# RWKV-5 recurrence into a SoLU feed-forward block on one core: w loaded from ScalarE's queue, one join behind the states' updates, and another order of the last steps

## The chip, the core and the metric

The kernel runs on one core of one Trainium2 chip. The metric is the device time in microseconds of one execution. The engines are named as the profile names them: PE is TensorE (PEld its weight loads), DVE is VectorE, ACT is ScalarE, POOL is GpSimd, SP is SyncE, which issues nearly all transfers here.

## What is computed

Shapes: batch 4, 8 heads, 768 steps, head width 48; the feed-forward block has 3072 rows of 384 and an inner width of 1024. All is float32, except that the feed-forward weights arrive as 64-bit words and are converted in the kernel.

```python
for t in range(S):                                   # B, H, S, D = 4, 8, 768, 48
    kt, vt, rt = k[:, :, t], v[:, :, t], r[:, :, t]
    cur = einsum('bhd,bhe->bhde', u * kt, vt)
    y[:, :, t] = einsum('bhd,bhde->bhe', rt, state + cur)
    state = w * state + einsum('bhd,bhe->bhde', kt, vt)
x = y.transpose(0, 2, 1, 3).reshape(B * S, H * D)    # 3072 x 384
h = x @ w_in                                         # 3072 x 1024
solu = h * softmax(h)
ln = (solu - mean(solu)) / sqrt(var(solu) + 1e-6) * g_ln
out = ln @ w_out                                     # 3072 x 384
```

## The kernel before

The sequence is cut into 6 chunks of 128 steps; with 4 batches this makes N = 24 units, and unit i carries the state of unit i - 4 on. A unit's 128 rows go through three stages that run at the same time for different units: the recurrence for units i and i + 1, the inner product and softmax for unit j = i - 2, and the output product for unit l = i - 7. The order of every engine is written out by hand (`manual_schedule`): each engine executes its instructions in the order in which the program lists them, and waits on semaphores for those of other engines. Tiles of one pool and tag take turns in a few buffers, and an instruction that writes into a buffer waits until the tile before is done with. The tag "raw" (6 buffers) holds loads of weights at first, later the halves described below.

**Start.** `w` (4 x 2 x 48) is loaded into `wq` by a transfer that POOL issues (L493); `u` into one row of `u_bc` by one that ACT issues (L496). POOL then makes an identity matrix, with which PE does three warming products (`spin`, L619), transposes w (`wd_ps`, L636) and spreads u over all rows by a product with ones (`u_ps`, L638, copied by ACT, L639). From `wd_ps` DVE builds powers `pw` and, by doubling, the table `tab` of decays for 128 steps (L643 to L654). The first products of POOL (`wide` L1313, `weigh` L734 and L735, `decay_k` L721), the scaling of the transposed r and k (L779, L790) and `kdec` come from this table.

**Middle.** From unit 9 on, k and r are turned by a transposing transfer of 16-bit halves: ACT splits the words into halves (L1133, L1139), SP issues the transfer (L1107), and DVE joins the halves again (`join_rk`, L1112, into a tile `big`). The normalised rows go the same way: `halve_ln` (ACT, L1118), L1107, `join_ln` (DVE, L1112). In each turn of the loop (i = 9, 11, 13, 15, 17) `first` is unit i + 2 and `second` unit i + 3. From l = 4 (`SEVEN`) two output blocks are computed together with seven block products instead of eight; this needs sums of rows (`row_sums_12`, DVE, L1192 and L1193; `row_sums_34`, L1197 and L1198) and differences of weights (`weight_sums`, L1182). The third difference overwrites weights in place, in the turn i = 11, on DVE. In such a turn `both_a` to `both_d` issue PE's block products (L1202) and what takes them out of PSUM: copies by ACT (L1219, L1230, L1235, L1278) and additions by DVE (L1228; `both_c`: L1262 and L1267). A block product that writes a bank again waits for the copy or addition that read it. `unit_a` (DVE, L1049 and L1053) multiplies the inner rows by their softmax, after ACT's exponential (L977); `update` (DVE, L949) writes the states.

**End.** After the loops the rest is listed step by step. For the last unit `unit_b` squares on ACT (L1061), `deviation` computes the variance, its power -1/2, and a scale and a shift on POOL:

```python
nc.gpsimd.tensor_scalar(out=var, ...)                # L1073
nc.gpsimd.tensor_tensor(out=rstd, ..., op=ALU.pow)   # L1075
nc.gpsimd.tensor_scalar(out=scale, ...)              # L1079
nc.gpsimd.tensor_tensor(out=shift, ...)              # L1081
```

`normalise` applies them on ACT (L1093), and halving, transposing and joining follow before the output products. Beside this, `check_next` reads the weights once more: it issues one load (SP, L524) and has ACT take the magnitudes of the load before (`mag`, L582); `check_least` takes their minimum on DVE (L590), and `compare_sums` (L691 to L700) and `check_sums` (one product `n_ps`, L706) turn all of it into a flag.

Of the kernel before, what the change touches and what calls it, by code (L numbers as in the profile page):

```python
# [12 lines left out]
ALU = mybir.AluOpType  # L13
# [386 lines left out]
def direct_path(  # L400
# [29 lines left out]
    nc = tc.nc  # L430
    B, H, S, D = r.shape
# [58 lines left out]
    w_out_sb = const.tile([128, KF, dm], F32, name="w_out_sb")  # L490
    decays = const.tile([128, HP], F32, name="decays")

    nc.gpsimd.dma_start(out=wq[:, :, 0:D], in_=w.rearrange("(a q) d -> a q d", q=2))  # L493
    nc.vector.memset(wq[:, :, D:], 1.0)
    u_row = u_bc[0:1].rearrange("p h d -> p (h d)")
    nc.scalar.dma_start(out=u_row, in_=u.rearrange("h d -> (h d)").unsqueeze(0))  # L496
# [571 lines left out]
        unit_a(i)  # L1068
        unit_b(i)

    def deviation(i, j):
        ss, var, rstd = (stats[:, n, i:j] for n in (2, 3, 4))
        nc.gpsimd.tensor_scalar(out=var, in0=ss, scalar1=1.0 / dff, scalar2=1e-6 * dff ** 2,  # L1073
                                op0=ALU.mult, op1=ALU.add)
        nc.gpsimd.tensor_tensor(out=rstd, in0=var, in1=neg_half.to_broadcast([128, j - i]), op=ALU.pow)  # L1075
        i = max(i, SEVEN)
        if i < j:
            tot, shift, scale, rstd = (stats[:, n, i:j] for n in (1, 2, 3, 4))
            nc.gpsimd.tensor_scalar(out=scale, in0=rstd, scalar1=-float(dff), scalar2=1.0,  # L1079
                                    op0=ALU.mult, op1=ALU.mult)  # L1080
            nc.gpsimd.tensor_tensor(out=shift, in0=tot, in1=rstd, op=ALU.mult)  # L1081

    def normalise_late(i):
        if SEVEN <= i < N:
# [4 lines left out]
    def normalise(i):  # L1089

        if SEVEN <= i < N:
            solu = live[i]["solu"]
            nc.scalar.activation(out=solu, in_=solu, func=ACT.Identity,  # L1093
                                 scale=stats[:, 3, i : i + 1], bias=stats[:, 2, i : i + 1])
# [26 lines left out]
    def join_ln(i):  # L1121
        X = live[i]
        if i not in ROOM:
            X["lnT"] = fpool.tile([128, KF, 128], F32, name="lnT")
        else:
            X["lnT"] = bigs[ROOM[i]].rearrange("p (f t) -> p f t", f=KF)
        join(X["lnT"], X["turned"])
# [19 lines left out]
    def join_rk(i):  # L1147
        X = factors(i)
        join(X["rk"].rearrange("p e a t -> p (e a) t"), X["turned"])
# [96 lines left out]
    def both_c_sum(i, also=False):  # L1246
        X = live[i]
        o2 = X["o2"]
        nc.vector.tensor_tensor(out=o2[:, right], in0=X["a"], in1=o2[:, right], op=ALU.add)
        X["summed"] = True  # L1250
        if also:
            o = X["o"]
            nc.vector.tensor_tensor(out=o[:, right], in0=X["e"], in1=o[:, right], op=ALU.add)
            X["summed"] = 2

    def both_c(i):
        X, Y = live.pop(i), live.pop(i + 1)
        ending[i] = X
        o, o2, a, e = (X[n] for n in ("o", "o2", "a", "e"))
        rows, rows2 = (out[ds(b * S + c * T, T)] for b, c in (units[i], units[i + 1]))  # L1260
        if not X.get("summed"):
            nc.vector.tensor_tensor(out=o2[:, right], in0=a, in1=o2[:, right], op=ALU.add)  # L1262
        block(a, Y["lnT"][:, KH:KF], sums_w[4])
        if i + 2 == N:
            nc.sync.dma_start(out=rows2[:, right], in_=o2[:, right])
        if X.get("summed") != 2:
            nc.vector.tensor_tensor(out=o[:, right], in0=e, in1=o[:, right], op=ALU.add)  # L1267
        nc.sync.dma_start(out=rows, in_=o)

    def both_d(i):  # L1270
        X = ending.pop(i)
        (b, c), o2, a = units[i + 1], X["o2"], X["a"]
        rows2 = out[ds(b * S + c * T, T)]
        if i + 2 == N:
            nc.vector.tensor_copy(out=o2[:, left], in_=a)
            nc.sync.dma_start(out=rows2[:, left], in_=o2[:, left])
        else:
            nc.scalar.copy(out=o2[:, left], in_=a)  # L1278
            nc.sync.dma_start(out=rows2, in_=o2)
# [177 lines left out]
    i = LA + LO  # L1457
# [42 lines left out]
    for i in range(LA + LO + 2, ELEVEN, 2):  # L1500
        j, l = i - LA, i - LA - LO
        seven = l >= SEVEN
        for n in (i + 6, i + 7):
            if n < N:
                load(n, "kr")
        for n in (i + 3, i + 4):
            if n < N:
                load(n, "v")
        deviation(j - 2, j)
        first, second = ([n] if n < N else [] for n in (i + 2, i + 3))  # L1510
        for n in first + second:
            diagonal(n)
        if SEVEN <= l <= EARLY:
            row_sums_34(l, nc.gpsimd)
        if l < SEVEN:
            decay(i + 4)
        elif i + 4 < N:
            weigh(i + 4, nc.gpsimd)
        decay(i + 5)
        if SEVEN <= l + 2 and i + 6 < N:  # L1520
            decay_k(i + 6)
            decay_r(i + 6)
        ffn_in(j)
        attend([i, i + 1])
        unit_a(j)
        second_pair = i == LA + LO + 2
        if l == EARLY + 4:
            check_next()
        if l < EARLY + 4:
            halve_ln(l + 2)  # L1530
        else:
            normalise(l + 3)
        if seven:
            both_a(l)
        if l == EARLY + 4:
            halve_ln(l + 3)
        for n in (i, i + 1):
            if n < N:
                place(n)
        if i >= CHECKED and l < EARLY + 4:  # L1540
            check_next()
        unit_b(j)
        if l == EARLY + 4:
            deviation(j, j + 1)
        if l <= EARLY:
            normalise(l + 3)
        take([i, i + 1])
        if second_pair:
            halve_rk(i + 3)
        if seven:  # L1550
            take_a(l, "DVE")
        else:
            join_ln(l + 1)
        if l == SEVEN:
            weight_sums((3,))
        check_least()
        for n in first:
            join_rk(n)
        if second_pair:
            weight_sums((4,))  # L1560
        if i + 4 < N:
            halve_rk(i + 4)
        if l == EARLY + 4:
            check_next()
        if seven:
            take_a(l, "ACT")
        else:
            ffn_out(l)
        if l > EARLY:
            turn_next(l + 3 if l < EARLY + 4 else l + 4)  # L1570
        ffn_in(j + 1)
        if seven:
            both_b(l)
        unit_a(j + 1)
        if seven:
            both_c(l)
        if l > EARLY:
            check_least()
        if l <= EARLY:
            halve_ln(l + 3)  # L1580
        else:
            turn_next(l + 4 if l < EARLY + 4 else l + 5)
        if l > EARLY:
            check_next()
        if seven:
            both_d(l)
        if l == EARLY + 4:
            join_ln(l + 2)
            join_ln(l + 3)
        if i + 4 == ELEVEN:  # L1590
            input_sums((1, 2), nc.vector)
        for n in (i, i + 1):
            if n < N:
                update(n, i + 2 < ELEVEN)
        for n in second:
            join_rk(n)
        if not seven:
            ffn_out(l + 1)
        for n in (i + 4, i + 5):
            if n < N:  # L1600
                sum_own(n)
        for n in (i, i + 1):
            if n < N:
                merged_y(n)
                take_y(n)
        if i + 2 == ELEVEN:
            eleven_a(j + 2)
        if l > EARLY:
            check_least()
        elif i >= CHECKED - 2:  # L1610
            check_next()
        unit_b(j + 1)
        if l == EARLY + 4:
            deviation(j + 1, j + 2)
        if l <= EARLY:
            normalise(l + 4)
        halve_rk(i + 5)
        if l < EARLY + 4:
            join_ln(l + 2)
            if i + 2 == ELEVEN:  # L1620
                take_first(j + 2)
            if l + 2 >= SEVEN:
                join_ln(l + 3)
        if l + 2 >= SEVEN:
            row_sums_12(l + 2)
        if l + 2 > EARLY:
            row_sums_34(l + 2, nc.vector)
        check_least()
# [150 lines left out]
    both_b(l)  # L1779
    unit_a(i)  # L1780
    unit_b(i)
    deviation(i, N)
    halve_ln(j + 1)
    both_c_sum(l)
    both_c(l)
    join_ln(l + 2)
    join_ln(l + 3)
    row_sums_12(l + 2)
    row_sums_34(l + 2, nc.vector)
    both_d(l)  # L1790
    both_a(l + 2, (0,))
    normalise(i)
    halve_ln(i)
    check_next()

# [2 lines left out]
    both_a(l, (1, 2))  # L1798
    take_a(l, "DVE")
    take_a(l, "ACT")  # L1800
    join_ln(l + 2)
    both_b(l)
    check_least()
    both_c(l)
    both_d(l)
    check_next()
    join_ln(l + 3)
    row_sums_12(l + 2)
    check_least()

    l += 2
    both_a(l)
    take_a(l, "DVE")
    take_a(l, "ACT")
    check_least()
    compare_sums()
    row_sums_34(l, nc.vector)
    both_b(l, check_sums)
    both_c(l)
    both_d(l)  # L1820
# [43 lines left out]
```

## Time and profile before

| | |
|---|---|
| median of 3 runs | 325.33 us (325.25 to 325.44) |
| the profiled execution | 326.05 us |
| its span, first to last instruction | 324.3 us |
| busy: PE, DVE, ACT, POOL | 308.9, 264.6, 245.0, 250.9 us |
| granted TensorE clock | 0.998 |
| DMA moved | 52.64 MB, 162 GB/s on average |

Starts are counted from the first instruction. In the chain of waits a line is start, duration and what it was; "issue" is time in which the engine waited for nothing that the profile shows. In the timeline a line is start, duration, engine, line, operation, tiles (written <- read), shape, and in brackets the idle time before it with what ended it.

### The profile page before, as it was taken

What the parts mean: (1) busy time and instruction counts of PE and PEld (TensorE: products, weight loads), DVE (VectorE), ACT (ScalarE), POOL (GpSimd) and SP (SyncE); (2) the same over time, 40 slices, a digit from 0 to 9 for tenths busy, and PEclk for the clock granted to TensorE, in tenths of its full rate; (3) what the DMA queues carried; (4) which work ended last, traced back from release to release, by engine and by line L of the source; (5) the groups of instructions that cost most, each with busy time, mean ns of one, the idle gap of its engine ahead of it and who ended that gap; (6) DMA issues with size and microseconds to landing.
All of it is one profiled execution on the core that took longest, in us unless ns stands there. A gap on an engine that the chain in (4) does not pass through costs nothing.

```text
span 324.3 us, 9699 instructions
## 1 busy us (share of the span) xinstructions
PE 308.9 (95%) x3903; PEld 216.7 (67%) x3903; DVE 264.6 (82%) x446; ACT 245.0 (76%) x418; POOL 250.9 (77%) x268
## 2 busy tenths in 40 slices
PE   5999999999999999999999999999999999999972
PEld 3875566555456457677678668668677676779972
DVE  6796999998887979999788699789979945868570
ACT  2875888888559788868968969949969978786410
POOL 4899878889999999999999999979978274275000
PEclk9999999999999999999999999999999999999999
DMA  8999999479999998996999999986757535674821
GB/s 165 255 255 200 207 244 169 75 140 139 194 169 173 174 183 144 159 193 106 167 186 164 176 195 225 197 171 133 143 152 161 92 103 147 144 172 102 166 91 61
DMA packets 165800, 52.64 MB, mean 162 GB/s; under 512 B 158321, under 2 KB 161522, under 8 KB 165746
## 3 DMA queue, kind: packets, MB, share of 16 engines
q1 hardware_dynamic: 165712, 51.92, 82.2%
q8 instruction: 33, 0.54, 0.7%
q14 instruction: 21, 0.17, 0.2%
q0 software_dynamic: 32, 0.00, 0.0%
q10 hardware_dynamic: 2, 0.00, 0.0%
HBM read 26.75 MB, written 4.72 MB: 97 GB/s over the span
## 4 chain that ended last, share of the span: by engine, by line
PE 58%; POOL 17%; DVE 12%; issue 5%; DMA 3%; ACT 2%; SPq 0%; POOLq 0%; ACTq 0%; DVEq 0%
PE o_ps L1202 22%; PE h_ps L969 16%; PE h_part L1003 9%; POOL rp L728 3%; POOL rku L734 3%; POOL big L754 3%; POOL kp L721 3%; PE y_ps L881 2%; PE at L819 2%; POOL rku L735 2%; DVE solu L1053 2%; DVE big L832 2%; DMA raw<-in_moe_w_out_dram 1%; PE y_ps L858 1%; PE h_part L881 1%
## 5 line engine op out<-in xcount | busy, mean ns | idle before, releaser
L969 PE MATMUL h_ps<-w_in_sb,xT 128*128 128x512 f32 x216 | 97.0, 598 | 0.0
L969 PEld LDWEIGHTS h_ps<-w_in_sb,xT 128*128 128x128 f32 x216 | 39.9, 190 | 45.1 <-issue 42.4
L1118 ACT COPY halves<-solu 128x2048 uint16<-128x2048 uint16 x23 | 43.6, 1897 | 1.2 <-DVE stats L1049 1.1
L1112 DVE COPY big<-halves 128x2048 uint16<-128x2048 uint16 x21 | 33.7, 1612 | 2.9 <-DMA halves<-halves 2.7
L721 POOL TENSOR_TENSOR kp<-kpad,kdec 128x512 f32<-128x512 f32 x24 | 34.1, 1423 | 0.7
L1112 DVE COPY lnT<-halves 128x2048 uint16<-128x2048 uint16 x18 | 30.1, 1684 | 1.5 <-DMA halves<-halves 1.4
L735 POOL TENSOR_TENSOR rku<-rku,rpad 128x384 f32<-128x384 f32 x24 | 29.0, 1210 | 1.9
L832 DVE COPY_PREDICATED big<-later_half,at 64x512 f32<-64x512 uint32 x40 | 29.4, 736 | 0.7
L734 POOL TENSOR_TENSOR rku<-kpad,u_bc 128x384 f32<-128x384 f32 x24 | 29.8, 1240 | 0.2
L754 POOL TENSOR_SCALAR_AFFINE_SELECT big<-own 64x512 f32<-64x512 f32 x40 | 27.7, 692 | 1.8
L1202 PE MATMUL o_ps<-w_out_sb,ma 128*128 128x192 f32 x160 | 28.1, 328 | 0.0
L1202 PEld LDWEIGHTS o_ps<-w_out_sb,ma 128*128 128x128 f32 x160 | 26.2, 190 | 1.9 <-issue 1.6
L728 POOL TENSOR_TENSOR rp<-rpad,rdec 128x512 f32<-128x512 f32 x15 | 25.5, 1703 | 0.0
L977 ACT ACTIVATE e<-h_ps 128x1024 f32<-128x1024 f32 x18 | 18.4, 1022 | 8.7 <-PE h_ps L969 8.6
L1073 POOL TENSOR_SCALAR stats<-stats 128x1 f32<-128x1 f32 (+2 forms) x14 | 7.2, 516 | 22.7 <-ACT e L1061 22.0
L1061 ACT ACTIVATE e<-solu,stats 128x1024 f32<-128x1024 f32 x20 | 23.0, 1148 | 2.1 <-DVE solu L1053 2.1
L1053 DVE SCALAR_TENSOR_TENSOR solu<-h_ps,stats,e 128x1024 f32<-128x1024 f32 x18 | 23.1, 1284 | 1.5
L1093 ACT ACTIVATE solu<-solu,stats 128x1024 f32<-128x1024 f32 x17 | 21.0, 1232 | 2.4 <-POOL stats L1081 2.4
L1157 PE MATMUL o_ps<-w_out_sb,lnT 128*128 128x384 f32 x64 | 21.6, 491 | 0.0
L1202 PE MATMUL o_ps<-w_out_sb,lnT 128*128 128x192 f32 x112 | 19.8, 330 | 0.0
L956 POOL TENSOR_TENSOR vt<-vt,wide 48x384 f32<-48x384 f32 x16 | 19.1, 1210 | 0.8
L1202 PEld LDWEIGHTS o_ps<-w_out_sb,lnT 128*128 128x128 f32 x112 | 18.3, 190 | 1.6 <-issue 1.4
(196 smaller groups left out, 703.6 us busy)
## 6 DMA issues: line engine op xcount, KB each, us to landing
raw<-in_moe_w_out_dram SPq DMA_DIRECT2D x16, 384.0 KB, 4.1
kpad<-in_k_dram SPq DMA_DIRECT2D x24, 192.0 KB, 5.0
rpad<-in_r_dram SPq DMA_DIRECT2D x24, 192.0 KB, 5.0
vt<-in_v_dram SPq DMA_DIRECT2D x40, 96.0 KB, 3.7
raw<-in_moe_w_in_dram SPq DMA_DIRECT2D x7, 512.0 KB, 6.3
out_dram<-o SPq DMA_DIRECT2D x18, 192.0 KB, 3.1
raw<-in_moe_w_in_dram SPq DMA_DIRECT2D x10, 256.0 KB, 3.4
out_dram<-kp SPq DMA_DIRECT2D x5, 192.0 KB, 3.0
```

What stands on the lines that cost most here:

```text
L721: nc.gpsimd.tensor_mul(X["kp"].rearrange("p h d -> p (h d)"), kpads[i % NLD].rearrange("p h d -> p (h d)"), kdec.rearrange("p a d -> p (a ...
L728: nc.gpsimd.tensor_mul(X["rp"].rearrange("p h d -> p (h d)"), rpads[i % NLD].rearrange("p h d -> p (h d)"), rdec.rearrange("p a d -> p (a ...
L734: engine.tensor_mul(rku, kpads[i % NLD][:, :, 0:D], u_bc)
L735: engine.tensor_mul(rku, rku, rpads[i % NLD][:, :, 0:D])
L754: nc.gpsimd.affine_select(out=G[rows, c].rearrange("p a q u -> p (a q) u"), in_=X["own"][rows].to_broadcast([U, H, U]), compare_op=ALU.is_ ...
L832: nc.vector.copy_predicated(X["G"][rows, c].rearrange("p a q u -> p q a u"), later_half[rows].unsqueeze(1).to_broadcast([U, 2, HP, U]), X[ ...
L969: nc.tensor.matmul(h_ps[:, ts(n, NX)], X["xT"][:, j, :], w_in_sb[:, j, ts(n, NX)], start=(j == 0), stop=(j == KD - 1))
L1003: nc.tensor.matmul(dst, rows, weights, start=start, stop=True, skip_group_check=True)
L1053: nc.vector.scalar_tensor_tensor(out=solu, in0=X["h"], scalar=rs, in1=X["e"], op0=ALU.mult, op1=ALU.mult, accum_out=tot)
L1112: nc.vector.tensor_copy(out=words.bitcast(U16).rearrange("p n (t o) -> p o n t", o=2), in_=turned)
L1118: copy(out=both.rearrange("p (o n) -> p o n", o=2), in_=split(X["solu"]))
L1202: nc.tensor.matmul(dst, rows[:, f], weights[:, f], start=(start and f == 0), stop=(f == KH - 1), skip_group_check=True)
```

## The change

Three places change. The transfer of w is issued by ACT, ahead of that of u, and no longer by POOL. In the turn with l == SEVEN the join of `first` is listed behind the updates, together with that of `second`. In the end, `deviation` is split into three functions; for the last unit the variance, scale and shift are done by DVE and only the power by POOL, one `join_ln` comes ahead of them, the last `normalise` ahead of the copy in `both_a`, a `join_ln` behind `both_b`, the last `check_next` stands behind the copies of the last stage's `both_a`, and `row_sums_34` comes ahead of the checks. (For the other units `deviation` issues what it did.) On PE and SP the order of instructions is the same in both programs.

```diff
-    nc.gpsimd.dma_start(out=wq[:, :, 0:D], in_=w.rearrange("(a q) d -> a q d", q=2))
+    nc.scalar.dma_start(out=wq[:, :, 0:D], in_=w.rearrange("(a q) d -> a q d", q=2))
...
-    def deviation(i, j):
-        ss, var, rstd = (stats[:, n, i:j] for n in (2, 3, 4))
-        nc.gpsimd.tensor_scalar(out=var, in0=ss, scalar1=1.0 / dff, scalar2=1e-6 * dff ** 2,
-                                op0=ALU.mult, op1=ALU.add)
-        nc.gpsimd.tensor_tensor(out=rstd, in0=var, in1=neg_half.to_broadcast([128, j - i]), op=ALU.pow)
+    def variance(i, j, engine):
+        engine.tensor_scalar(out=stats[:, 3, i:j], in0=stats[:, 2, i:j], scalar1=1.0 / dff,
+                             scalar2=1e-6 * dff ** 2, op0=ALU.mult, op1=ALU.add)
+
+    def root(i, j):
+        nc.gpsimd.tensor_tensor(out=stats[:, 4, i:j], in0=stats[:, 3, i:j],
+                                in1=neg_half.to_broadcast([128, j - i]), op=ALU.pow)
+
+    def shifts(i, j, engine):
         i = max(i, SEVEN)
         if i < j:
             tot, shift, scale, rstd = (stats[:, n, i:j] for n in (1, 2, 3, 4))
-            nc.gpsimd.tensor_scalar(out=scale, in0=rstd, scalar1=-float(dff), scalar2=1.0,
-                                    op0=ALU.mult, op1=ALU.mult)
-            nc.gpsimd.tensor_tensor(out=shift, in0=tot, in1=rstd, op=ALU.mult)
+            engine.tensor_scalar(out=scale, in0=rstd, scalar1=-float(dff), scalar2=1.0,
+                                 op0=ALU.mult, op1=ALU.mult)
+            engine.tensor_tensor(out=shift, in0=tot, in1=rstd, op=ALU.mult)
+
+    def deviation(i, j):
+        variance(i, j, nc.gpsimd)
+        root(i, j)
+        shifts(i, j, nc.gpsimd)
...
         check_least()
-        for n in first:
-            join_rk(n)
+        if l != SEVEN:
+            for n in first:
+                join_rk(n)
...
                 update(n, i + 2 < ELEVEN)
-        for n in second:
+        for n in first + second if l == SEVEN else second:
             join_rk(n)
...
     unit_a(i)
     unit_b(i)
-    deviation(i, N)
     halve_ln(j + 1)
     both_c_sum(l)
+    join_ln(l + 2)
+    variance(i, N, nc.vector)
+    root(i, N)
     both_c(l)
-    join_ln(l + 2)
+    shifts(i, N, nc.vector)
     join_ln(l + 3)
     row_sums_12(l + 2)
     row_sums_34(l + 2, nc.vector)
     both_d(l)
+    normalise(i)
     both_a(l + 2, (0,))
-    normalise(i)
     halve_ln(i)
     check_next()
 
     l += 2
     live[l]["copy"] = nc.vector.tensor_copy
     both_a(l, (1, 2))
     take_a(l, "DVE")
     take_a(l, "ACT")
+    both_b(l)
     join_ln(l + 2)
-    both_b(l)
     check_least()
     both_c(l)
     both_d(l)
-    check_next()
     join_ln(l + 3)
     row_sums_12(l + 2)
-    check_least()
 
     l += 2
     both_a(l)
     take_a(l, "DVE")
     take_a(l, "ACT")
+    check_next()
+    row_sums_34(l, nc.vector)
     check_least()
     compare_sums()
-    row_sums_34(l, nc.vector)
     both_b(l, check_sums)
```

## The prediction

> **What bounds the kernel now.** I read the page's busy shares and slices first, then the chain of waits in order of time, then the timeline of each engine around the three places that the diff touches.
>
> ```profile
> PE 308.9 (95%) x3903; PEld 216.7 (67%) x3903; DVE 264.6 (82%) x446; ACT 245.0 (76%) x418; POOL 250.9 (77%) x268
> PE   5999999999999999999999999999999999999972
> PE 58%; POOL 17%; DVE 12%; issue 5%; DMA 3%; ACT 2%; SPq 0%; POOLq 0%; ACTq 0%; DVEq 0%
> ```
>
> TensorE is busy 95% of the span and carries 58% of the chain; POOL carries 17%, between 67 and 122 us. TensorE's idle time lies in the first slice, in a few tenths before 141 us, and at the end. The diff leaves TensorE's instructions and their order as they are, so it can gain only where TensorE waits.
>
> The chain at the start:
>
> ```profile
> 1.45 3.75 DMA wq<-in_w_dram
> 5.19 0.14 issue
> 5.33 0.25 PE wd_ps L636
> 5.58 0.02 issue
> 5.60 0.16 DVE pw L643
> ...
> 8.03 0.70 DVE tab L654
> ```
>
> Nothing but the transfer of w holds the first 5.2 us: the table of decays (DVE, 5.60 to 8.73) starts when w has landed, and POOL's first products (9.41) and all later work start from the table.
>
> The third weight difference (DVE L1182, 134.97) is in the iteration i = 11. Timelines of three engines:
>
> ```profile
> 140.17 1.57 PE L1202 MATMUL o_ps<-lows,lnT 128*128 128x192 f32 x8 [0.52 <-DVE o L1262]
> 136.28 2.12 DVE L1112 COPY big<-halves 128x2048 uint16<-128x2048 uint16 x1
> 139.76 0.35 DVE L1262 TENSOR_TENSOR o<-o_ps,o 128x192 f32<-128x192 f32 x1
> 138.50 1.90 ACT L1118 COPY halves<-solu 128x2048 uint16<-128x2048 uint16 x1 [1.09 <-DVE stats L1049]
> ```
>
> The join of r and k (2.12 us) stands before DVE's unit and before the addition L1262, for which TensorE waits 0.52 us. ACT's copy for row block 7 waits for the same join.
>
> The end of the chain:
>
> ```profile
> 296.30 2.27 POOL stats L1073
> 298.65 1.09 POOL stats L1075
> ...
> 300.73 1.25 ACT solu L1093
> 302.01 1.90 ACT halves L1118
> ...
> 304.46 1.26 SPq L1107
> 305.81 4.49 DMA raw<-in_moe_w_out_dram
> 310.38 0.65 ACT mag L582 x2
> ...
> 311.28 4.17 PE o_ps L1202 x24
> ```
>
> The last block's statistics take POOL from 296.30 to 300.70. Scaling, halving and the transposing DMA follow, and TensorE waits 1.64 us before its last stage (311.28). Two things end there together: the join and sums of the last block (DVE L1193 ends 311.03), and ACT's copy of the sums (310.93 to 311.22), which stood behind a check (L582) that waited for its own load of weights, landed at 310.30.
>
> **What the skill says.** The Trainium skill, "DMA: Bandwidth & Descriptors", SWDGE vs HWDGE vs iDMA: a DMA issued from GpSimd has its descriptors written by software there; one from ScalarE has them from hardware, with a faster setup. The trace agrees: the w load holds POOL 0.81 us and lands 3.75 us after its start, while u on ScalarE's queue (0.51 us of issue from 0.80) released ScalarE at 2.13, 1.33 us after its start. The skill, "SBUF — State Buffer", SBUF: two separate sides: VectorE in a two-port mode and GpSimd share a port pair that one holds for a whole instruction. That fits the 2.27 us of POOL's L1073 beside DVE's two joins (296.00 to 298.53), where the same instruction took 0.19 at 291.39.
>
> **Part 1, w by ScalarE.** POOL loses the issue. It began at 1.45 and held back the identity (2.26 to 2.85) and with it TensorE's three spin products (2.91 to 4.56). POOL's queue was released at 0.69, so the identity is done near 1.4 and the spins near 3.1. ScalarE issues w at 0.80 and u at 1.31; by u's 1.33, w lands near 2.1 and u near 2.6. u's delay of 0.5 goes on to the activation table's load (1.28 us, then done near 4) and is hidden: the first use of it is the copy of u at 7.09, which follows TensorE's product. The transpose of w then starts near 3.1 instead of 5.33, and DVE, busy with memsets until 3.67, starts the table at about 3.7 instead of 5.60: 1.9 us earlier.
>
> Does that pass on? Landings, from the DMA view: r of unit 0 at 5.0, its transpose would move from 6.98 to 5.1; r of unit 1 at 9.7, used at 12.44; weights 5 at 21.9, used at about 23.4, so late by 0.4 after the move, on an ACT that is 0.75 us ahead of DVE's L827 there (ends 26.5, used 27.28). Later loads land 2.5 us and more before their use. From 58 to 64.7 us SP waits for ACT (7.9 us), so DMA is not the pace there, and everything after is released by engines. I take **1.8 us**, ends 0.6 (w takes the 3.75 of the old path from 0.80) and 1.9.
>
> **Part 2, the join behind the updates.** DVE's L1049 then waits for ACT's exponential (ends 136.96) instead of the join: unit 137.0 to 138.5, L1262 at about 138.6, after TensorE's block has ended (138.2). TensorE continues at 139.65: 0.52 gained. Given back: L1267 needs the block that ends at 139.65, so DVE idles 0.8, and the joins of 13 and 14 follow the updates (141.5 to 145.6) where one alone ended at 143.89. Both are wanted by the score products at 148.9 only. DVE is then 1.0 us late with the sums L1193 (151.87, now about 152.9), which TensorE wants at 153.46 less 0.5: nearly even, at most 0.1 lost; the next waits of DVE in that iteration (1.78 us for ACT) take the rest up. The buffers change with the order: ACT's copy for block 7 takes the buffer of block 6, whose transposing DMA (issued 134.57, 4.7 us to landing) ends at 139.3 instead of the join's 138.5. Behind that copy on ACT stand L1278 (1.38 us idle before it) and the copies of y that TensorE's 143.60 needs; the 0.8 fits in the idle time. Its own transposing DMA, on SP, starts at 141.9 instead of 140.9 and lands near 148.2, when DVE gets to it (148.3). I take **0.4**, ends -0.3 and 0.5.
>
> **Part 3, the end.** The variance (L1073) and the two shifts go to DVE, the power stays on POOL, and one join comes ahead. DVE: addition to 295.1, join 295.1 to 296.4 (its data landed at 290.7), variance at once since ACT's square ends at 296.22. Power on POOL from 296.6, with DVE nearly idle 0.56 us as at 291.66 (1.09 if not), then two shifts of some 0.15 each: done near 297.5 instead of 300.70. ACT is busy with the former halves until 298.0 and copies L1278 to 298.2, so the scaling runs 298.2 to 299.5, the copy L1219, moved behind it, to 299.75, the halving to 301.65 instead of 303.9. SP is free at 301.5. The transposing DMA, with the 4.3 us from 303.93 to the join's 308.25, lands at 306.0; join and sums end at 309.0 instead of 311.03.
> What that costs: the other join of this stage waits for the shifts (from 297.27 to 297.5), so its sums are ready at 300.3 and L1228 at 301.75 instead of 301.52: TensorE's stage slips by 0.2 to 0.25. The 0.39 that it saves before the stage (join at 296.4) is lost in this wait. It reaches the last stage at 309.9, where sums (309.0) and L1219 (308.7) are ready. The last check's read on ACT now follows L1230 (311.5 to 312.2); its minimum, the comparisons and their reduction on DVE end at 313.5, and TensorE wants them at 313.8. DVE's sums 3 and 4, put ahead, are there at 311.5, wanted at 312.5. From 309.9 the last stage is as long as before: 311.28 - 309.9 = **1.4**, ends 0.6 and 2.0. SP's order is the same in both programs: the last step of the checks only reads, it issues no load.
>
> **Sum:** 1.8 + 0.4 + 1.4 = 3.6 us. The profiled execution took 326.05 (span 324.3 and 1.75 around it), which becomes 322.4; the median of the runs is 325.33, which becomes **321.7**. About 0.2% (0.65 us) is what a measurement of this kernel can tell from no change.
>
> **Rivals.**
> *The start does not pass on.* The DMA line is at 8 and 9 for the first 60 us; if loads set the pace, engines only wait for them later. Against it: no engine's wait in that stretch is ended by a load but that of w and u. Gain 1.8, time 323.5. Chance 0.13.
> *The end turns into a new wait.* If the power meets a DVE copy (1.09 or 2.3 instead of 0.56), the second join and TensorE's stage slip by 0.5 to 1.7 more and little of 1.4 is left. Against it: DVE waits for the power itself. Gain 2.2 to 2.9, time about 322.9. Chance 0.10.
> *Slower: w lands behind the first loads.* SP's loads issued at 2.80 and 3.28 took 5.8 and 6.4 us. If w and u on ScalarE's queue take 6.4 from 0.80 and 1.31, they land at 7.2 and 7.7; the product of u starts 2.3 us later than its 5.44, and all behind it. With +1.8 from the rest: 325.33 + 2.4 - 1.8 = 325.9. It decides from a landing of w near 7. Against it: u, issued in the same instant as the first load, took 1.33. Chance 0.04.
> *The change does less than it says* (buffers or semaphores put the same waits elsewhere, parts 2 and 3 near nothing, w no earlier than the spins): within 0.65 us, 325.2. Chance 0.03.
>
> **Numbers.** My forecast (3.0 to 4.2 us gained) has 0.70. Range 320.8 to 323.6: from 1.9 + 0.5 + 2.0 to the rival without the start. Faster 0.93, same 0.03, slower 0.04.
>
> **What would show it.** wd_ps near 3.2 and the first table step near 3.7; POOL's first product near 7.6; no wait before TensorE's L1202 in the middle; in the end POOL's power of about 0.6, the last transposing DMA issued near 2.2 us earlier against the stage before it, and no wait for ACT's copy before the last stage. A table that starts after 5, or TensorE's first large product (23.54) not 1.5 earlier, would prove part 1 wrong; a new wait of TensorE over 0.5 us after 141 parts 2 or 3.

## The result, and the profile after

The kernel after takes **322.65 us** (median of 6 runs, 321.68 to 323.85), the kernel before 325.46 us in the same comparison (6 runs, 325.25 to 326.10): ratio 0.9903, 95% interval 0.9885 to 0.9920. That is 2.6 to 3.7 us gained, 2.8 by the medians; 3.6 and a time of 321.7 were predicted. The time lies in the predicted range (320.8 to 323.6), the 2.8 just under the 3.0 to 4.2 that had the highest chance. Executions over 1.5% slower than the fastest of their kernel (two of stats_pool's 22, below) are left out of the ratios. The profiled execution took 322.73 us, with a span of 321.0.

The page of the kernel after, with the lines that answer to the first ones of before:

```profile
PE 307.4 (96%) x3903; PEld 216.9 (68%) x3903; DVE 265.9 (83%) x449; ACT 244.4 (76%) x418; POOL 245.6 (77%) x264
PE   6989999999999999999999999999999999999992
PE 61%; POOL 18%; DVE 10%; issue 4%; DMA 3%; SPq 1%; ACT 0%; POOLq 0%; ACTq 0%
```

TensorE executes the same 3903 products, with 307.4 us of busy time instead of 308.9; the other 1.8 us of the 3.3 that the span lost were idle. The 7 near the end of its slices has become a 9, the first slice a 6. Line numbers behind the function `deviation` are now 9 higher (L1202 is L1211, L1262 is L1271, L1112 is L1121), L1073 and L1075 are L1072 and L1076.

The start, in the timeline (start, duration, engine and line, operation, tiles, and in brackets the idle time before it and what ended it):

```profile
0.79 1.27 ACTq L493 DMA_DIRECT2D wq<-in_w_dram  x1
2.10 0.27 ACTq L496 DMA_DIRECT2D u_bc<-in_u_dram  x1
4.38 0.24 PE L636 MATMUL wd_ps<-ident,wq 4*128 4x4 f32 x1 [1.33 <-DMA wq<-in_w_dram]
4.66 0.16 DVE L643 TENSOR_SCALAR pw<-wd_ps 128x4 f32<-128x4 f32 x1 [1.00 <-PE wd_ps L636]
4.88 1.28 ACT L639 ACT_TABLE_LOAD   x1 [4.88 <-DMA u_bc<-in_u_dram]
4.95 1.61 PE L638 MATMUL u_ps<-u_bc,ones_row 1*128 1x384 f32 x2 [0.32 <-DMA u_bc<-in_u_dram]
6.59 0.48 ACT L639 COPY u_bc<-u_ps 128x384 f32<-128x384 f32 x1 [0.43 <-PE u_ps L638]
10.09 0.57 ACT L665 COPY kdec<-kd_ps 128x512 f32<-128x512 f32 x1
10.74 2.52 POOL L721 TENSOR_TENSOR kp<-kpad,kdec 128x512 f32<-128x512 f32 x2 [0.20 <-ACT kdec L665]
```

The table starts at 4.66 instead of 5.60, 0.94 us earlier and not 1.9: w was on its way for 3.46 us (0.79 to 4.25 in the chain of waits). And u, behind it on ScalarE's queue, released ScalarE at 4.88 instead of 2.13, and TensorE waits 0.32 us for it before `u_ps`. `kdec` comes only 0.50 us earlier than in before (10.59 there), and POOL waits for it.

The middle, same view:

```profile
136.42 0.17 DVE L1049 RECIPROCAL stats<-sums 128x1 f32<-128x1 f32 x1 [0.64 <-ACT e L977]
137.90 0.35 DVE L1271 TENSOR_TENSOR o<-o_ps,o 128x192 f32<-128x192 f32 x1
138.58 1.90 ACT L1127 COPY halves<-solu 128x2048 uint16<-128x2048 uint16 x1 [1.75 <-DMA halves<-halves]
138.91 1.46 PE L1211 MATMUL o_ps<-lows,lnT 128*128 128x192 f32 x8
139.11 0.36 DVE L1276 TENSOR_TENSOR o<-o_ps,o 128x192 f32<-128x192 f32 x1 [0.86 <-PE o_ps L1211]
```

TensorE's block of 138.91 (140.17 in before) follows the one ahead of it with no wait; DVE now waits 0.86 us instead.

The end of the chain of waits (start, duration, what):

```profile
293.51 1.25 DVE big L1121
...
295.67 1.25 DVE big L1121
...
298.51 13.39 PE o_ps L1211 x80
311.89 0.12 PE n_ps L706 x2
312.01 2.81 PE o_ps L1211 x16
```

From 298.51 on TensorE runs without a wait to its last block; the 1.64 us before the last stage is gone. One wait is new, in the timeline:

```profile
298.51 1.54 PE L1211 MATMUL o_ps<-lows,ma 128*128 128x192 f32 x8 [0.56 <-DVE ma L1202]
```

It stands for one that went: before had 0.39 us at 297.37, for the join that now comes first.

To see what each place gave I match TensorE's instructions of two traces and take the difference of their starts (each from its first instruction). Medians over stretches, in us against before, for all kernels below:

| kernel | 35 to 60 | 141 to 200 | 218 to 290 | last stage |
|---|---|---|---|---|
| after | -0.55 | -1.32 | -1.61 | -3.55 |
| start_alone | -0.55 | -0.55 | -1.09 | -1.77 |
| middle_alone | +0.07 | -0.73 | -1.30 | -1.33 |
| end_alone | +0.32 | +0.32 | +0.19 | -1.74 |
| w_pool_late | -0.04 | -0.79 | -1.05 | -2.99 |
| u_first | +0.09 | -0.73 | -0.87 | -2.79 |
| w_sp | -1.13 | -1.88 | -2.01 | -3.94 |
| u_sp | -1.59 | -2.36 | -3.22 | -5.13 |
| r_first | -1.55 | -2.36 | -2.08 | -3.99 |
| k_act | -1.45 | -2.27 | -3.29 | -5.22 |
| check_alone | -0.04 | -0.07 | -0.73 | -1.51 |
| stats_alone | -0.10 | -0.09 | -0.65 | -2.59 |
| stats_pool | -0.42 | -1.34 | -1.61 | -2.83 |

In the kernel after the start gave 0.55, the middle 0.77 and the end 1.94. The step between 141 to 200 and 218 to 290 is no part of the change: see the stall in the last section. Of the end's 1.94, 0.6 to 0.7 may belong to the one traced execution of before (POOL, same section).

### The profile page after: what moved, and what is told of

It is laid out like the page before. It is cut to its first block, busy times and chain, and to the rows that moved or that the text cites. A ratio compares the mean times of both kernels' runs of the same rounds, so it can differ in the third digit from the quotient of the medians.

```text
span 321.0 us, 9696 instructions
## 1 busy us (share of the span) xinstructions
PE 307.4 (96%) x3903; PEld 216.9 (68%) x3903; DVE 265.9 (83%) x449; ACT 244.4 (76%) x418; POOL 245.6 (77%) x264
## 4 chain that ended last, share of the span: by engine, by line
PE 61%; POOL 18%; DVE 10%; issue 4%; DMA 3%; SPq 1%; ACT 0%; POOLq 0%; ACTq 0%
PE o_ps L1211 26%; PE h_ps L969 16%; PE h_part L1003 9%; POOL kp L721 4%; POOL rku L734 4%; POOL big L754 3%; POOL rp L728 3%; PE y_ps L881 2%; POOL rku L735 2%; PE at L819 2%; DMA vt<-in_v_dram 1%; DVE ma L552 1%; PE h_part L881 1%; DMA wq<-in_w_dram 1%; DVE big L832 1%
## 5 line engine op out<-in xcount | busy, mean ns | idle before, releaser
L721 POOL TENSOR_TENSOR kp<-kpad,kdec 128x512 f32<-128x512 f32 x24 | 34.1, 1423 | 0.9 <-ACT kdec L665 0.2
L1121 DVE COPY big<-halves 128x2048 uint16<-128x2048 uint16 x21 | 33.8, 1613 | 0.6 <-DMA halves<-halves 0.3
L1121 DVE COPY lnT<-halves 128x2048 uint16<-128x2048 uint16 x18 | 31.2, 1759 | 0.0
L734 POOL TENSOR_TENSOR rku<-kpad,u_bc 128x384 f32<-128x384 f32 x24 | 29.8, 1241 | 0.2
L1211 PE MATMUL o_ps<-w_out_sb,ma 128*128 128x192 f32 x160 | 28.1, 328 | 0.0
L1211 PEld LDWEIGHTS o_ps<-w_out_sb,ma 128*128 128x128 f32 x160 | 26.2, 190 | 1.9 <-issue 1.6
L1072 POOL TENSOR_SCALAR stats<-stats 128x2 f32<-128x2 f32 (+2 forms) x13 | 5.9, 451 | 19.2 <-ACT e L1061 18.7
L1211 PE MATMUL o_ps<-w_out_sb,lnT 128*128 128x192 f32 x112 | 19.8, 330 | 0.0
L1211 PEld LDWEIGHTS o_ps<-w_out_sb,lnT 128*128 128x128 f32 x112 | 18.2, 190 | 1.7 <-issue 1.4
```

The source lines that it names most:

```text
L721: nc.gpsimd.tensor_mul(X["kp"].rearrange("p h d -> p (h d)"), kpads[i % NLD].rearrange("p h d -> p (h d)"), kdec.rearrange("p a d -> p (a ...
L734: engine.tensor_mul(rku, kpads[i % NLD][:, :, 0:D], u_bc)
L1121: nc.vector.tensor_copy(out=words.bitcast(U16).rearrange("p n (t o) -> p o n t", o=2), in_=turned)
L1211: nc.tensor.matmul(dst, rows[:, f], weights[:, f], start=(start and f == 0), stop=(f == KH - 1), skip_group_check=True)
```

## The experiments

Ratios are to runs of before on the same chip: 34 runs with median 325.95 us beside start_alone, middle_alone, end_alone and w_sp; 33 with 325.61 beside check_alone, stats_alone, u_first and w_pool_late; 27 with 325.82 beside the other four.

**Each part alone.**

start_alone is before with the first edit only:

```diff
-    nc.gpsimd.dma_start(out=wq[:, :, 0:D], ...)
+    nc.scalar.dma_start(out=wq[:, :, 0:D], ...)
```

> Kernel before with one edit: the transfer of w issued by ACT ahead of that of u. Theory (parts add): the table of decays starts 0.94 us earlier, about 0.6 of it is left on PE after 25 us (a stall of PE with the releaser 'issue' near 21.6 grows from 0.2 to 0.7), and the time falls by about 0.6 us, ratio 0.998. Rival (swallowed): later loads or the stall take all of it, within 0.2 us of before. Rival (my forecast's size): 1.8 us, ratio 0.9945.

Measured: 325.0 us, ratio 0.9968 (0.9954 to 0.9982). The start passes on: by the times 1.0 us (0.6 to 1.5). In its trace the table starts 1.05 us earlier and TensorE is 0.55 earlier from 35 us on, so about half is lost on the way. There is no stall near 21 us at all, so the stall isn't what eats the rest (the kernel after has 0.73 us of it and the same 0.55). A loss is seen in POOL, which waits longer here, and in what it waits for:

```profile
5.16 1.61 PE L638 MATMUL u_ps<-u_bc,ones_row 1*128 1x384 f32 x2 [0.64 <-DMA u_bc<-in_u_dram]
6.81 0.48 ACT L639 COPY u_bc<-u_ps 128x384 f32<-128x384 f32 x1 [0.43 <-PE u_ps L638]
10.31 0.57 ACT L665 COPY kdec<-kd_ps 128x512 f32<-128x512 f32 x1
10.95 1.27 POOL L721 TENSOR_TENSOR kp<-kpad,kdec 128x512 f32<-128x512 f32 x1 [0.51 <-ACT kdec L665]
```

L721 began at 11.45 in before, 0.50 later; POOL's L734 before it had been 1.05 earlier (8.36 against 9.41). The half that is lost here is u's: TensorE's product `u_ps` waits 0.64 us for the late u and starts only 0.28 earlier than in before (5.44 there), and behind it come the copy of u, 3.2 us of fills on ACT (L641) and `kdec`. The table load is not in this chain: it ended at 6.37, and the copy waited until 6.81 for the product. That u is the whole of the loss up to 35 us was not tested by a run of its own.

middle_alone, before with the join of `first` behind the updates where l == SEVEN:

> Kernel before with one edit: the join of unit 13 listed behind the updates where l == SEVEN. Theory (parts add): PE's wait of 0.52 us before the block product at 140 goes, PE is about 0.7 us earlier from there to the end, 324.7 (ratio 0.998). Rival (given back): the wait comes back later, by the joins or by the next stage, 325.3 (ratio 1.000).

Measured: 325.25 us, ratio 0.9973 (0.9960 to 0.9985); TensorE is 0.80 us earlier behind that turn (-0.73 against +0.07) and nothing is given back later. The theory holds.

end_alone, before with the diff below `unit_b(i)` and the three functions:

> Kernel before with the end's new order alone (statistics on DVE, join and checks moved). Theory (parts add): PE's wait of 1.64 us before its last stage goes, a new one of about 0.6 comes at the stage before; 1.8 us gained, ratio 0.9945. Rival (needs the other parts): since the stage before waits for DVE's sums, the gain is under 1.0 us when all of the end starts later, ratio above 0.997.

Measured: 324.39 us, ratio 0.9948 (0.9929 to 0.9967), and 1.93 us on TensorE's last stage, with the new wait of 0.56 us at the stage before. The end needs no other part. The product of the three ratios is 0.9889, inside the interval of after, and in the traces 0.55 + 0.80 + 1.93 = 3.28 us stand against 3.26: the parts add.

**Which edit of the end?** check_alone is before with only the checks moved:

```diff
     both_d(l)
-    check_next()
     join_ln(l + 3)
     row_sums_12(l + 2)
-    check_least()
...
     take_a(l, "ACT")
+    check_next()
+    row_sums_34(l, nc.vector)
     check_least()
     compare_sums()
-    row_sums_34(l, nc.vector)
```

> Kernel before with only the last check_next behind the copies and row_sums_34 ahead of the checks; statistics and joins as before. Theory (two waits ended together before the last stage: DVE's sums at 311.03, ACT's copy at 311.22): the copy goes early, the sums stay, gain 0.2 us, ratio 0.9993. Rival (the copy behind the check was the wait): PE's wait of 1.64 us goes, gain 1.6, ratio 0.995.

Measured: 326.07 us, ratio 1.0013 (1.0002 to 1.0025). The rival, a gain of 1.6 us, is out; not even the 0.2 us shows. In its trace ACT's copy is early (307.61) and TensorE still waits, 0.92 us, for DVE's sums.

stats_alone, the end's new order with those five lines as before has them:

> Kernel before with the end's statistics on DVE and its joins moved, but check_next and check_least where before has them. Theory (two waits together): the sums come 1.8 us earlier, the copy still stands behind the check whose load landed at 310.3 (its issue by SP moves up with the transposing transfer ahead of it, so the load lands 1 to 2 us earlier if SP sets it, and not if it is held by the load's own time): gain 0.2 to 0.6 us if the load stays, ratio 0.998 to 0.9993. Rival (the load moves up with SP): gain 1.4 to 1.8, ratio 0.9945 to 0.9957, and the checks' move is worth nothing.

Measured: 323.96 us, ratio 0.9954 (0.9938 to 0.9970), the same as end_alone within the intervals. The rival was right and my theory wrong, in the timeline of stats_alone:

```profile
303.48 0.54 SPq L524 DMA_DIRECT2D raw<-in_moe_w_out_dram  x1
307.03 0.56 ACT L582 ACTIVATE mag<-raw 128x384 f32<-128x384 f32 x1 [0.33 <-DMA raw<-in_moe_w_out_dram]
307.69 0.32 ACT L1228 COPY kp<-o_ps 128x192 f32<-128x192 f32 x1
```

The check's load stands behind the transposing DMA on SP. When the statistics are early, that DMA and so the load go out 2.3 us earlier (305.81 in before), and the copy behind the check comes at 307.69 instead of 310.93, ahead of the stage at 308.79. The two waits had one cause, and on top of the other edits of the end the move of the checks is worth nothing.

stats_pool, after with the engine alone undone:

```diff
-    variance(i, N, nc.vector)
+    variance(i, N, nc.gpsimd)
...
-    shifts(i, N, nc.vector)
+    shifts(i, N, nc.gpsimd)
```

> Kernel after with the last unit's variance and two shifts on POOL again, at the same places; the rest of the end as in after. Theory (VectorE's joins slow POOL's small instructions, and this is what the end's gain removes): the four take 2.5 to 4.4 us on POOL instead of 1.0 on both, the scaling starts 1 to 2.5 later than in after, PE's wait before the second last stage (0.56) goes but one of 0.9 to 2.5 comes back before the last: 0.3 to 2.0 us above after, ratio to before 0.991 to 0.996. Rival (the order of join, scaling and copies carried the gain, not the engine): within 0.3 us of after, or 0.5 below since the second join waits for nothing.

Measured: 323.98 us, ratio 0.9941 (0.9926 to 0.9957) where after had 0.9903. In its trace the end gives 1.22 us instead of 1.94. The four instructions in stats_pool:

```profile
294.64 0.19 POOL L1072 TENSOR_SCALAR stats<-stats 128x1 f32<-128x1 f32 x1 [3.54 <-ACT e L1061]
294.91 1.67 POOL L1076 TENSOR_TENSOR stats<-stats,neg_half 128x1 f32<-128x1 f32 x1
296.67 0.39 POOL L1083 TENSOR_SCALAR stats<-stats 128x1 f32<-128x1 f32 x1
297.14 0.65 POOL L1085 TENSOR_TENSOR stats<-stats 128x1 f32<-128x1 f32 x1
```

and in after:

```profile
294.64 0.14 DVE L1072 TENSOR_SCALAR stats<-stats 128x1 f32<-128x1 f32 x1
294.86 0.55 POOL L1076 TENSOR_TENSOR stats<-stats,neg_half 128x1 f32<-128x1 f32 x1 [3.73 <-DVE stats L1072]
295.45 0.15 DVE L1083 TENSOR_SCALAR stats<-stats 128x1 f32<-128x1 f32 x1 [0.40 <-POOL stats L1076]
295.52 0.15 DVE L1085 TENSOR_TENSOR stats<-stats 128x1 f32<-128x1 f32 x1
```

Both begin at 294.64; on POOL beside DVE's join (294.89 to 296.2) and sums they take 3.15 us, on the two engines in turn 1.03. In after DVE begins its second join only when the power is there (it waits 0.40 us for it, with only an addition, 294.70 to 295.05, before), so no join runs beside the power, and it takes 0.55. The wait that comes back is 1.39 us before the second last stage, for ACT's copy L1228 that now stands behind the scaling, and not before the last stage as I expected. So within the new order the engine is worth 0.7 of the end's 1.9 us in the trace, some 1.2 by the times (0.9941 - 0.9903); the rest is order. The engine without the new order was not tried.

**Why did w need 3.46 us?** w_sp, after with w issued by SP ahead of all its loads:

```diff
-    nc.scalar.dma_start(out=wq[:, :, 0:D], ...)
...
+    nc.sync.dma_start(out=wq[:, :, 0:D], ...)
     load(0, "kr")
```

> Kernel after with w issued by SP ahead of unit 0's k and r, u still by ACT. Theory (two queues that issue at the same instant slow each other): w's issue takes 0.3 to 0.6 us, w lands 1.3 to 2.2 after its start (after: 3.46), the table starts near 3.7 instead of 4.66; k and r of unit 0 start 0.5 later. Time 0.3 to 0.7 us below after's if it passes on, equal to it if the stall of PE near 21.6 takes it. Rival (the shape of w's transfer costs it: short runs into 4 partitions): issue 1.27 and landing 3.46 again on SP, the table as in after, first loads later by 1.3, time as after's or up to 0.5 worse.

Measured: 321.19 us (5 runs, 320.71 to 322.01), ratio 0.9854 (0.9832 to 0.9877). w's issue took 0.86 us, TensorE transposed w at 2.99 without waiting for it, and the table began at 3.52. k and r of unit 0 landed 0.9 and 1.0 us later. By the ratios it is 1.6 us below after, more than the 0.3 to 0.7 that the theory had. So the shape of w's transfer doesn't cost the 3.46. Two issues in the same instant remain here too (u on ACT, 0.79), without harm, so my reason, that they slow each other, is not it either.

u_first, after with ACT's two transfers swapped:

> Kernel after with the two transfers of ACT swapped: u first, w behind it. Theory (w's issue of 1.27 us came from issuing in the same instant as SP's first load): from 1.30 w takes 0.5 to 0.9 us to issue, is there by 2.6 to 3.3, the table starts at about 3.6 as with w on SP, and the loads of unit 0 stay where after has them: time as w on SP or 0.3 us below, ratio to before 0.984 to 0.986. Rival (w's shape costs 1.27 us on ACT whenever it goes): w issued until 2.6, landed at 4.8 to 5.2, table later than in after by 0.3 to 0.5, ratio 0.991 to 0.993.

Measured: 323.76 us, ratio 0.9951 (0.9930 to 0.9973). w was issued from 1.36 in 0.76 us and still landed 3.7 us after its start (wd_ps at 5.16): the start's gain is gone (+0.09). Theory and rival both fail, for the issue was short and the landing was late. Some 1460 of SP's packets had begun when w's first did, at 3.38.

w_pool_late, after with w on POOL's queue behind the identity:

> Kernel after with w again on POOL's queue, but behind the identity. It parts the identity (and PE's spins) from w's own way. Theory (only w's landing matters): issued near 1.5, landed 3.75 later at 5.2 as in before, the table starts at 5.6, nothing of the start's gain is left: time 0.6 to 1.0 us above after's, ratio to before 0.992 to 0.993. Rival (the identity and spins carried the gain): table and time as after's.

Measured: 323.36 us, ratio 0.9937 (0.9918 to 0.9956). The spins are 1.5 us earlier as in after, w is used at 5.30, and the start gives 0.04. The identity and the spins carried nothing; w's landing is all.

u_sp, after with u on SP ahead of unit 0's k, and w alone on ACT's queue:

```diff
-    nc.scalar.dma_start(out=u_row, ...)
...
+    nc.sync.dma_start(out=u_row, ...)
     load(0, "kr")
```

> Kernel after with w on ACT's queue as its only load and u issued by SP ahead of unit 0's k. It asks why w on ACT's queue landed 3.5 us after its start and by 2.2 on SP's. Theory (w's packets, put on ACT's queue, lie behind those of k and r, issued by SP in the same instant; here k comes 0.5 later): w lands 1.8 to 2.5 after its start, the table starts at 3.5 to 3.7, time as with w on SP, ratio 0.985. Rival (ACT's queue is itself slower for w's twelve short runs): w again at 4.2 or later, the table at 4.6, ratio 0.990 to 0.991.

Measured: **320.41 us** (5 runs, 319.63 to 321.37), ratio 0.9846 (0.9832 to 0.9860). w's issue took 1.25 us as in after, and yet TensorE needed no wait for it at 2.99. Timeline of u_sp:

```profile
0.78 1.25 ACTq L493 DMA_DIRECT2D wq<-in_w_dram  x1
0.79 0.36 SPq L593 DMA_DIRECT2D u_bc<-in_u_dram  x1
2.15 1.28 ACT L639 ACT_TABLE_LOAD   x1 [2.15 <-DMA u_bc<-in_u_dram]
2.99 0.27 PE L636 MATMUL wd_ps<-ident,wq 4*128 4x4 f32 x1
3.52 0.15 DVE L643 TENSOR_SCALAR pw<-wd_ps 128x4 f32<-128x4 f32 x1
8.57 0.59 ACT L665 COPY kdec<-kd_ps 128x512 f32<-128x512 f32 x1 [0.20 <-PE kd_ps L664]
9.37 1.28 POOL L721 TENSOR_TENSOR kp<-kpad,kdec 128x512 f32<-128x512 f32 x1
```

The DMA view of the first 2.8 us (queue, kind, packets, MB, share of the 16 engines; q1 is SP's queue, q10 ACT's), after:

```profile
DMA  0000000000000000000000000002456896999999
q1 hardware_dynamic: 797, 0.15, 28.6%
```

and u_sp:

```profile
DMA  0000000000000000000000000000000000021485
q1 hardware_dynamic: 147, 0.03, 5.8%
q10 hardware_dynamic: 12, 0.00, 0.3%
```

In after k's packets begin at 1.90; when w's first packet begins at 2.86, some 870 of SP's have begun and the engines' line is at 9. w's last packet begins at 3.13, and w has landed at 4.25. In u_sp only u's two packets (from 1.72) are ahead, w's twelve (eight with data) begin between 2.34 and 2.41, and k's from 2.47. So w lands late where its packets come behind those of k and r: the 0.4 us by which u's issue holds back k's on SP makes the difference. Whether w's packets wait in the DMA engines or are written late beside k's, these traces don't tell. That u and w land by 2.15 and 2.99 also ends ACT's late chain (`kdec` 8.57 against 10.09).

**Better versions.** u_sp has the lowest ratio of this study: by the two ratios 0.9942 of after, some 1.9 us, and the intervals don't touch. In the traces it is 1.6 us, of which 0.5 is the stall at 214 us that u_sp didn't have. From w_sp, r_first and k_act it can't be told by the times. The last two were built on w_sp.

r_first, unit 0's r ahead of its k:

> The kernel with w on SP, and r of unit 0 loaded ahead of its k (there PE's first transpose waited 1.36 us for r, landed at 5.97, while k was there at 4.93). Theory: r at about 4.95, DVE's first product with the table at 6.65 instead of 7.23, 0.3 to 0.6 us earlier to the first unit; by 28 us PE is at most 0.3 earlier, since with w on SP ACT and DVE already wait there for the loads of weights (1.73 and 0.68 us): 320.9 to 321.2, ratio to before 0.985 to 0.986. Rival (the start still sets everything): 0.6 us all the way, ratio 0.9835.

Measured: 321.26 us (320.31 to 323.33), ratio 0.9876 (0.9851 to 0.9902). The first product with the table came at 6.75, TensorE at 35 us was 0.4 earlier than in w_sp (-1.55 against -1.13), more than the theory had; a stall of 1.06 us at 213 then took most of it in this execution. By the times it can't be told from w_sp.

k_act, unit 0's k issued by ACT behind u:

```diff
+    nc.scalar.dma_start(out=kpads[0][:, :, 0:D], in_=k[...])
-    load(0, "kr")
+    load(0, "r")
```

> The kernel with w on SP, and k of unit 0 issued by ACT behind u, so SP's other loads are issued 0.45 us earlier. Theory (in the kernel with w on SP the loads of weights are the pace near 20 us, by their issue on SP): r at 5.0 to 5.5, weights 0.4 earlier, PE at 28 us 0.3 to 0.5 earlier, 320.7 to 320.9, ratio 0.984. Rival (the DMA engines are the pace, not the issue): loads land as before, time as with w on SP or 0.3 above since ACT's queue delivers k later.

Measured: 321.3 us (4 runs), ratio 0.9865 (0.9851 to 0.9879). The trace has the 0.3 us at 35 us (-1.45), the times don't show it. Inconclusive.

## Why the prediction was right, and where it was not

**Bound and sign: right.** TensorE's idle time at three places was all there was to gain, and each part gave some of it. 3.6 us were forecast, 2.8 measured by medians and 3.3 in the spans. That the sum came so close was in part luck: in the traces part 1 fell short by 1.25 us, parts 2 and 3 gave 0.9 more than I had put, and 0.3 of the 3.3 is the stall.

**Part 1, 1.8 forecast, 0.55 in the trace (1.0, from 0.6 to 1.5, by start_alone's times): two terms were wrong.** The sign that I had set for this came: TensorE's first large product (23.54 in before) was to start 1.5 earlier and started 0.21 earlier, at 23.33, with 0.55 more of the stall ahead of it than in before. "by u's 1.33, w lands near 2.1" took the price of a transfer whose packets ran ahead of SP's for one whose packets ran behind some 870 of them: 3.46. The end that I had set at 3.75 "from 0.80" was nearly what happened, and my value should have stood nearer to it. "u's delay of 0.5 goes on to the activation table's load ... and is hidden" was wrong in size and in path: u was 2.75 us later (4.88). The table load was indeed hidden (done at 6.16, the copy of u at 6.59). But TensorE's product of u stands directly behind that of w: it waited 0.32 us for u (0.64 in start_alone), and the copy of u, ACT's fills and `kdec`, which POOL waited for, came after it. I had followed u on ScalarE's queue and not to TensorE. The other steps held: identity at 1.35, spins from 1.41, the table at once behind w. (SP's wait that ends at 64.67 is 6.3 us in the timeline, from 58.4, and not 7.9; nothing rests on its length.) That it passes on if w is early was right too: u_sp begins the table 2.08 earlier and keeps 1.6.

**Part 2, 0.4 forecast, 0.77 measured: right, mis-sized.** DVE's unit, the wait for ACT's exponential, the 0.86 us of DVE before L1276, ACT's copy held by the DMA of block 6 and the joins behind the updates are all as written. The "0.52 gained" was too small by 0.16: in the trace a block that follows without a wait begins 0.16 before the modelled end of the one ahead (305.23 + 2.76 = 307.99, and the next begins at 307.83), so an idle time of 0.52 is worth 0.68. And the 0.1 that I took for DVE's late sums did not come.

**Part 3, 1.4 forecast, 1.94 measured: right, mis-sized.** The same 0.16 makes the 1.64 us worth 1.80. That the stage before "slips by 0.2 to 0.25" did not come about (TensorE was 0.08 earlier there), as DVE's shifts and sums were ready 0.2 to 0.3 earlier than I had put it. By its length the new wait of 0.56 us is the sign that I had set against parts 2 and 3 (over 0.5), but the 0.39 saved before that stage is in it, as forecast. The Trainium skill, "SBUF — State Buffer", SBUF: two separate sides, has VectorE in a two-port mode and GpSimd share a port pair, which one of them holds for a whole instruction. The traces fit that: 0.55 us for the power with no join of DVE beside it, 1.67 with one. But the cause I gave for half of the old wait, the check in ACT's queue, was no cause of its own (check_alone, stats_alone).

**Rivals.** "The start does not pass on" came nearest: not because DMA set the pace later, but because w and u were late. w behind the first loads is what happened in kind, at 4.25 and not 7, so it did not decide the sign.

**The queue.** The Trainium skill, "DMA: Bandwidth & Descriptors", SWDGE vs HWDGE vs iDMA, says that a hardware queue sets up faster than GpSimd's. Here the hardware queue took 3.46 us against 3.75, with SP's packets ahead of w's in both (some 870 in after, 1090 in before); with w's ahead of k's the hardware queue took at most 2.2. GpSimd's queue with nothing ahead was not tried.

## What to carry to other kernels

Price a small transfer at the head of a kernel by which packets are ahead of its own, and not by its queue alone: here the hardware queue needed 3.46 us with some 870 packets that another queue had begun in the 1 us before, and at most 2.2 with two. When a transfer is put ahead of another on a queue, follow the second one to every engine that uses it, and through what that engine does next. If two waits end together, ask whether one step releases both before an edit is made for each.

## What the runs showed of the hardware that was not expected

TensorE has two stalls whose releaser is "issue", in `y_ps` near 21 and 214 us, and their length seems to belong to the execution, not to the kernel. start_alone and after issue the same up to 130 us; the first has none at 21, the second this:

```profile
21.63 0.30 PE L858 MATMUL y_ps<-big,vt 128*32 128x128 f32 x2 [0.73 <-issue]
213.86 0.64 PE L881 MATMUL y_ps<-big,vt 128*32 128x64 f32 x28 [0.47 <-issue]
```

Before had 0.18 and 0.77, r_first 0.65 and 1.06. Spans of single executions are therefore no better than about 1 us, and times of several runs have to decide. The traces hold a likely cause. Both stalls stand before the same two products in every trace that has them, and each ends 2.3 to 2.8 us after a packet of 16,384 bytes, which the DMA view counts as "instruction" (queue q8), has begun: at 19.27 for the 21.63 of after, at 211.05 for the 213.86. In no trace does one of these two products start sooner than 2.2 us after such a packet, and where the packet is early (210.68 in end_alone, 4.1 us ahead) there is no stall. That fits a TensorE that waits for its next instructions. No run moved these packets, and what sets their start stays open.

POOL's four instructions on 128x1 numbers at the end of before took 4.4 us in some executions (before, middle_alone) and 3.8 in others, with DVE's joins beside them; check_alone:

```profile
295.53 1.05 POOL L1073 TENSOR_SCALAR stats<-stats 128x1 f32<-128x1 f32 x1 [3.53 <-ACT e L1061]
296.66 1.48 POOL L1075 TENSOR_TENSOR stats<-stats,neg_half 128x1 f32<-128x1 f32 x1
```

In before the same two took 2.26 and 1.08. start_alone, which edits nothing at the end and has the 3.8, shows 0.68 us between the last two columns of the table; middle_alone, with the 4.4, shows 0.03. So most of check_alone's 0.78 is this difference too, as its times show no gain. And as before was traced with the 4.4, the end's 1.94 would be about 1.3 against an execution with the 3.8 (an estimate, 1.94 - 0.68); by the times end_alone gained 1.7 us (1.1 to 2.3). The two differ in where POOL gets in: its first instruction ends 0.03 us after the second join in before (298.53), and 0.04 after the first in check_alone (296.54). What decides it stays open.
